# Gated linear attention and its feed-forward block: the first sequence's state held in compact form

## The chip, the cores and the metric

The kernel runs on one core of a Trainium2 chip. A core has five engines, each with an instruction queue of its own that it works through in order: TensorE (PE in the profile; PEld are its weight loads), VectorE (DVE), ScalarE (ACT), GpSimd (POOL) and SyncE (SP, which here issues every DMA). They meet only by semaphores. The metric is device time in microseconds (us), the median of several runs; smaller is better.

## The reference

Four sequences (b) of 768 tokens, 8 heads (h), 48 numbers per head. Each head carries a 48 x 48 state that decays per row by a gate f and takes in one outer product per token; the output of a token is its query times the state. The outputs, joined over the heads to 384 numbers per token, pass through a feed-forward block with a 3-tap convolution over the tokens.

```python
f = 1.0 / (1.0 + np.exp(-f_logit))
for t in range(S):
    state = f[:, :, t, :, None] * state + np.einsum('bhd,bhe->bhde', k[:, :, t], v[:, :, t])
    y[:, :, t] = np.einsum('bhd,bhde->bhe', q[:, :, t], state)
...
x = np.ascontiguousarray(attn_out.transpose(0, 2, 1, 3)).reshape(B, S, H * D)
h = np.maximum(x @ w_in, 0.0)
...
for k in range(K):
    conv_out += conv_w[k][None, None, :] * hp[:, k:k + S, :]
gate = 1.0 / (1.0 + np.exp(-conv_out))
return (h * gate @ w_out).astype(np.float32)
```

## The kernel before, in words

**Chunks.** Each sequence is cut into 6 chunks of 128 tokens; n = 0 to 23 numbers them over all four sequences, and (b, c) are the sequence and the chunk's place in it. Inside a chunk the recurrence becomes matrix products. The 8 heads go in 4 pairs p, and the two heads of a pair (j = 0, 1) lie on partitions 0 to 47 and 64 to 111. `HP` is 64, `D` is 48, `NP` is 4. On the host q and k are padded with zeros from 48 to 64 numbers per head.

**Stages of a chunk.** `gate` takes Exp and Ln of the forget logits (`fb`). `stage_a` sums them along the tokens with a triangular matmul, takes both exponentials (`fi`, `fd`, L213 and L214) and scales k and q (L226, L227). `stage_b` transposes k and q on TensorE and copies them out of PSUM (`kT`, `qT`, L251). `scores` makes the 128 x 128 score blocks (L291) and masks them with one predicated copy (`am`, L293). `state` makes the chunk's k-by-v products `pk` (L305), adds the old state (`stmp`, L315) and multiplies by the chunk's decay `ft` (L316, or L312 for the first chunk of a sequence). `values` multiplies the query block by the old state (L328) and the masked scores by v (L331) into one PSUM tile `py`, which is copied out as a high and a low part (`xT`, L339 and L340).

**The state's layout.** A state tile (`st`, two of them, `s_b[n % 2]`) has for each pair 112 columns. The head of j = 0 sits in rows 0 to 47 and columns 0 to 47, the head of j = 1 in rows 64 to 111 and columns 64 to 111; all else is zero. So one matmul of 128 rows by 112 columns per pair gives both heads' products (L328), while the update has to write the two blocks one after the other: per chunk two instructions L315 and two L316, each of 48 partitions by 192 numbers.

**The feed-forward block** is split in 8 units of half a sequence. `mm1` (L368) multiplies by w_in and does Relu, convolution and tanh on ScalarE and VectorE (L371 to L383); `mm2` (L398 to L409) splits the result into a high and a low part and multiplies by w_out (L405). The weights arrive as 64-bit floats and are split on chip (`split_f64`, L101 to L123; the tiles `mswi` and `mswo`). This happens beside the attention of the first sequence.

**What sets the order.** `plan` gives every piece a due time by hand and the pieces are recorded in that order. A scheduler then reorders the instructions of each engine by dependences and by its own estimate of the times. For chunks from n = 8 on, `visit` pins the attention's matmuls in a fixed order; before that the scheduler is free. All DMAs stand in SP's one queue: loads of k, q, v and of the logits (`load_f`, L174), the rows of the decay for later chunks (`decay_out`, `decay_in`, L233 and L241), the moves of `xT` (L345) and the output.

Of the kernel before, what the change touches and what calls it, by code (L numbers as in the profile page):

```python
# [9 lines left out]
F32 = mybir.dt.float32  # L10
# [5 lines left out]
ALU = mybir.AluOpType  # L16
PSUM = bass.MemoryType.PSUM
P = 128
# [1 line left out]
F64_HI = float(np.uint32((1151 << 20) - 1).view(np.float32))  # L20

F_MIN = 2.0 ** -64
CFG = dict(ez="ddddddaaaavvvv", ng=8, hp=4000, tb=2, groups=[3, 3, 3, 3, 3, 3, 3, 3], sg=3, f1=2.6, g1=2.6, gv=2, gl=5.2, g=3.9, l=3.2, a=1.8, b=0.8, s=0.2, v=0.5, wil=(-2.3, -1.1), wis=(-0.7, 0.9), cw=1.3, wol=(1.3, 1.0), wos=2.1, wo=0.35, m1=0.5, m1s=0.9, m2=1.5, m2s=1.2, ek=(12, 24), ec='d', er='p', tp=0, tf=2, nw=2, gd=0, q0=2, lf=3, kpool=2, eg='d', eq='p', es='d', em='d', ew='p', xb=3, nf=6, fe='a', kb=4, qb=3, vb=4, lv=2.2, cb=1, sb=3, fi=1)

@with_exitstack
def gla_moe_kernel(ctx, tc, q_in, k_in, v_in, f_in, w_in, conv_w, w_out, out):


    nc = tc.nc
    B, S, H, D = v_in.shape  # L30
    DM, DFF = w_in.shape
    q, k, v, f_logit = [t.rearrange("b s h d -> b h s d")[:, :, :, :D] for t in (q_in, k_in, v_in, f_in)]
    NC = S // P
    NP = H // 2
# [3 lines left out]
    CPH = NC // 2  # L38
    groups = CFG["groups"]
    GC = max(groups)  # L40
    first = [sum(groups[:g]) for g in range(len(groups) + 1)]
    WC = 512
    steps = [(b, c) for b in range(B) for c in range(NC)]
    HP = 64
    GAP = HP - D
# [6 lines left out]
    wk = fast.enter_context(tc.tile_pool(name="wk", bufs=2))  # L52
# [21 lines left out]
    def zeroed(shape, n, name, eng):  # L74
        ts = [wk.tile(shape, F32, name=f"{name}{i}", bufs=1) for i in range(n)]
        for t in ts:
            eng.memset(t, 0.0)
        return ts

    kp_b = [wk.tile([P, H, HP], F32, name=f"kp{i}", bufs=1) for i in range(CFG["kb"])]  # L80
    qp_b = [wk.tile([P, H, HP], F32, name=f"qp{i}", bufs=1) for i in range(CFG["qb"])]
    a_b = zeroed([P, 2, NP, P], 2, "am", nc.vector)
    s_b = zeroed([P, NP, HP + D], 2, "st", nc.vector)
# [3 lines left out]
    ft_all = const.tile([P, B, NC, NP], F32, name="ft_all")  # L87
    nc.gpsimd.memset(ft_all, 1.0)
    wi = const.tile([P, KT, 2, DFF], F32R, name="wi")
    wo = const.tile([P, NF, 2, DM], F32R, name="wo")  # L90
    cw = const.tile([P, 3, NF], F32, name="cw")

    def split_f64(raw, n, hi, lo, nm, tile=0):

        pr = raw.rearrange("p (n w) -> p n w", w=2)
        lw, hw = pr[:, :, 0], pr[:, :, 1]
        r = raw.shape[0]
        ms = wk.tile([P, 2, WC], I32, tag="gl", name=f"ms{nm}")
        m, s = ms[:r, 0, :n], ms[:r, 1, :n]
        mf, sf = m.bitcast(F32), s.bitcast(F32)  # L100
        nc.scalar.activation(mf, hw.bitcast(F32), AF.Abs)  # L101
        nc.vector.tensor_scalar(mf, mf, F64_LO, F64_HI, ALU.max, ALU.min)
        nc.vector.tensor_scalar(m, m, 1 << 27, 3, ALU.bitwise_xor, ALU.logical_shift_left)
        nc.scalar.activation(mf, mf, AF.Abs)
        nc.vector.scalar_tensor_tensor(m, hw, -(1 << 31), m, ALU.bitwise_and, ALU.bitwise_or)
        nc.vector.tensor_scalar(s, m, -(1 << 23), None, ALU.bitwise_and)
        if lo is None:
            nc.vector.scalar_tensor_tensor(sf, lw.bitcast(U32), 2.0 ** -52, sf, ALU.mult, ALU.mult)
            nc.vector.tensor_tensor(hi, mf, sf, ALU.add)
# [8 lines left out]
        nc.vector.scalar_tensor_tensor(low, lw.bitcast(U32), 2.0 ** -52, sf, ALU.mult, ALU.mult)  # L118
# [12 lines left out]

    def raw_out(f):
        i = f // 4
        if ("o", i) not in raws:
            raws["o", i] = (wk.tile([P, 4, 2 * DM], I32, tag="g32", name=f"wos{i}") if i == 0 else
                            wk.tile([P, 4, 2 * DM], I32, tag="xT", name=f"wos{i}", bufs=CFG["xb"]))
        return raws["o", i][:, f % 4]

    def load_w_in(kt, i):
        nc.sync.dma_start(raw_in(kt, i), w_in[kt * P:(kt + 1) * P, i * WC:(i + 1) * WC].bitcast(I32))  # L140

    def split_w_in(kt, i):
        cs = slice(i * WC, (i + 1) * WC)
        split_f64(raw_in(kt, i), WC, wi[:, kt, 0, cs], wi[:, kt, 1, cs], f"wi{kt}_{i}", KT * i + kt)
# [150 lines left out]
    def state(n):  # L295
        b, c = steps[n]
        if c == NC - 1:
            return
        kp, kT, qT = tts[n]
        vt = qkv[n]  # L300
        pk = ps.tile([P, NP, D], F32, tag="s", name=f"pk{n}", bufs=3)
        with visit(n - 1, 1):
            for p in range(NP):
                for j in range(2):
                    nc.tensor.matmul(pk[HP * j:HP * j + D, p, :], kp[:, 2 * p + j, :D], vt[:, 2 * p + j, :],  # L305
                                     start=True, stop=True)
        for j in range(2):
            r = slice(HP * j, HP * j + D)
            ft = ft_all[r, b, c, :].rearrange("p (n o) -> p n o", o=1).broadcast_to([D, NP, D])
            new = s_b[(n + 1) % 2][r, :, HP * j:HP * j + D]  # L310
            if c == 0:
                nc.vector.tensor_tensor(new, pk[r], ft, ALU.mult)  # L312
            else:
                tmp = wk.tile([P, NP, D], F32, tag="stmp", name=f"stmp{n}_{j}", bufs=1)
                nc.vector.tensor_tensor(tmp[r], pk[r], s_b[n % 2][r, :, HP * j:HP * j + D], ALU.add)  # L315
                (nc.vector if CFG["es"] == "d" else nc.gpsimd).tensor_tensor(new, tmp[r], ft, ALU.mult)  # L316

    def values(n):
        b, c = steps[n]
        kp, kT, qT = tts.pop(n)  # L320
        vt = qkv.pop(n)
        am = a_b[n % 2]
        py = ps.tile([P, NP, P], F32, tag="Y", name=f"py{n}")
        inter = c > 0 or n == 0
        with visit(n, 0):
            if inter:
                for p in range(NP):
                    nc.tensor.matmul(py[:HP + D, p, :], s_b[n % 2][:, p, :], qT[:, p, :], start=(p == 0), stop=False)  # L328
            for p in range(NP):
                for j in range(2):  # L330
                    nc.tensor.matmul(py[HP * j:HP * j + D, p, :], vt[:, 2 * p + j, :], am[:, j, p, :],  # L331
                                     start=not inter and p == 0, stop=(p == NP - 1))
        hf = c // CPH
        if c % CPH == 0:
            xts[b, hf] = wk.tile([P, NP, 2, HS], F32R, tag="xT", name=f"xT{b}_{hf}", bufs=CFG["xb"])
        xT = xts[b, hf]
        ts = slice((c % CPH) * P, (c % CPH + 1) * P)
        for r in [slice(0, HP + D)] if c > 0 or n == 0 else [slice(0, D), slice(HP, HP + D)]:
            nc.scalar.copy(xT[r, :, 0, ts], py[r])  # L339
            nc.vector.tensor_tensor(xT[r, :, 1, ts], py[r], xT[r, :, 0, ts].bitcast(F32), ALU.subtract)  # L340
# [133 lines left out]
    with tc.If(n_ok < P * n_ft):  # L474
        with ExitStack() as slow:
            wk = slow.enter_context(tc.tile_pool(name="swk", bufs=2))
# [13 lines left out]
            for t0 in range(0, S, TB):  # L490
# [7 lines left out]
                fb, qb, kb = grouped(f_logit, "f"), grouped(q, "q"), grouped(k, "k")  # L498
                vb = wk.tile([P, TB, D], F32, tag="sv", name=f"sv{t0}")
# [22 lines left out]
                for t in range(0, TB, 8):  # L522
                    py = ps.tile([B * H, 8, D], F32, tag="sy", name=f"spy{t0}_{t}", bufs=2)
# [14 lines left out]
            for u in range(2 * B):  # L538
                b, hf = u // 2, u % 2
# [59 lines left out]
```

## Time and profile before

| | |
|---|---|
| median of 3 runs | 376.55 us (374.24 to 377.16) |
| the profiled execution | 371.6 us, of which 369.9 us are the profile's span |
| PE busy | 346.4 us, 94% of the span |
| DVE busy | 290.4 us, 79% |
| ACT busy | 237.9 us, 64% |
| POOL busy | 53.0 us, 14% |

The span is the profile's stretch from its first to its last instruction. Busy shares are averages over stages with different limits: the first 110 us hold the weight splitting, the attention of the first sequence and the start of the feed-forward block, and only after that is TensorE filled throughout. A matmul's duration in a row holds its latency, and matmuls overlap; the busy time of a group divided by its count tells what one of them costs in a stream.

### The profile page before, as it was taken

What the parts mean: (1) busy time and instruction counts of PE and PEld (TensorE: products, weight loads), DVE (VectorE), ACT (ScalarE), POOL (GpSimd) and SP (SyncE); (2) the same over time, 40 slices, a digit from 0 to 9 for tenths busy, and PEclk for the clock granted to TensorE, in tenths of its full rate; (3) what the DMA queues carried; (4) which work ended last, traced back from release to release, by engine and by line L of the source; (5) the groups of instructions that cost most, each with busy time, mean ns of one, the idle gap of its engine ahead of it and who ended that gap; (6) DMA issues with size and microseconds to landing.
All of it is one profiled execution on the core that took longest, in us unless ns stands there. A gap on an engine that the chain in (4) does not pass through costs nothing.

```text
span 369.9 us, 7330 instructions
## 1 busy us (share of the span) xinstructions
PE 346.4 (94%) x2775; PEld 315.4 (85%) x2775; DVE 290.4 (79%) x455; ACT 237.9 (64%) x428; POOL 53.0 (14%) x72
## 2 busy tenths in 40 slices
PE   4799899989799998999999999999999999999993
PEld 1566678778699997999899999999999999999993
DVE  4799999999899877888689897689868875575620
ACT  3779777897977667567856566457464545665530
POOL 1111222112111410240101421041010000000000
PEclk9699999999999999999999999999999999999998
DMA  7999344315312450335113331341011002101011
GB/s 228 394 356 365 98 139 123 99 37 161 81 29 88 101 171 20 96 88 165 51 44 90 88 114 50 74 110 51 24 43 35 23 0 56 43 2 43 23 43 51
DMA packets 28853, 36.04 MB, mean 97 GB/s; under 512 B 10847, under 2 KB 20106, under 8 KB 28810
## 3 DMA queue, kind: packets, MB, share of 16 engines
q1 hardware_dynamic: 28810, 35.49, 32.1%
q8 instruction: 24, 0.39, 0.5%
q14 instruction: 19, 0.16, 0.1%
HBM read 28.37 MB, written 4.75 MB: 90 GB/s over the span
## 4 chain that ended last, share of the span: by engine, by line
PE 59%; ACT 14%; DVE 14%; DMA 6%; issue 4%; SPq 1%; ACTq 0%; DVEq 0%
PE po L405 23%; PE ph L368 20%; PE py L331 4%; DMA fb<-in_f_logit_dram 4%; PE pa L291 4%; PE py L328 3%; DMA wis<-in_moe_w_in_dram 2%; DVE g L379 2%; ACT fb L183 2%; DVE am L293 1%; PE ptk L249 1%; PE ptq L249 1%; PE pk L305 1%; ACT hb L371 1%; ACT g L373 1%
## 5 line engine op out<-in xcount | busy, mean ns | idle before, releaser
L368 PE MATMUL ph<-xT,wi 128*128 128x384 f32 x576 | 112.2, 344 | 4.5 <-ACT ob L408 2.5
L368 PEld LDWEIGHTS ph<-xT,wi 128*128 128x128 f32 x576 | 100.6, 188 | 8.2 <-ACT ob L408 3.7
L405 PE MATMUL po<-wo,gh 128*128 128x384 f32 x384 | 99.7, 340 | 0.2 <-ACT hb L371 0.2
L405 PEld LDWEIGHTS po<-wo,gh 128*128 128x128 f32 x384 | 69.6, 188 | 0.7 <-ACT hb L371 0.5
L405 PE MATMUL po<-wo,gl 128*128 128x384 f32 x192 | 66.0, 344 | 0.0
L379 DVE SCALAR_TENSOR_TENSOR g<-hb,cw,g 128x384 f32<-128x384 f32 (+1 forms) x64 | 43.5, 682 | 13.1 <-ACT g L373 12.5
L382 ACT ACTIVATE g<-g 128x768 f32<-128x768 f32 (+1 forms) x32 | 27.1, 848 | 38.7 <-DVE g L380 38.5
L371 ACT ACTIVATE hb<-ph 128x384 f32<-128x384 f32 x64 | 31.2, 489 | 23.5 <-PE ph L368 23.2
L380 DVE SCALAR_TENSOR_TENSOR g<-hb,cw,g 128x384 f32<-128x384 f32 (+1 forms) x64 | 41.8, 653 | 2.9
L399 DVE TENSOR_TENSOR gl<-g,gh 128x1024 fp32r<-128x1024 f32 (+4 forms) x34 | 32.2, 957 | 14.7 <-ACT gh L398 14.6
L383 DVE SCALAR_TENSOR_TENSOR g<-g,hb 128x768 f32<-128x768 f32 (+1 forms) x32 | 30.6, 957 | 14.1 <-ACT g L382 14.0
L227 POOL TENSOR_TENSOR qp<-qp,fd 128x384 f32<-128x384 f32 x22 | 28.9, 1313 | 87.7 <-ACT fd L214 72.1
L373 ACT ACTIVATE g<-hb,cw 128x384 f32<-128x384 f32 (+1 forms) x64 | 39.3, 619 | 2.2 <-ACT hb L371 0.4
L398 ACT CAST gh<-g 128x1024 fp32r<-128x1024 f32 (+4 forms) x34 | 26.5, 802 | 20.8 <-PE po L405 18.4
L405 PEld LDWEIGHTS po<-wo,gl 128*128 128x128 f32 x192 | 36.1, 188 | 1.1 <-issue 0.2
L293 DVE COPY_PREDICATED am<-mask,pa 128x1024 f32<-128x1024 uint8 x24 | 31.6, 1315 | 0.3
L291 PE MATMUL pa<-qT,kT 48*128 48x128 f32 x384 | 28.8, 286 | 0.4 <-ACT qT L251 0.4
L331 PE MATMUL py<-am,v 128*48 128x128 f32 x384 | 26.8, 277 | 1.6 <-DVE am L293 1.6
L226 DVE TENSOR_TENSOR kp<-kp,fi 128x384 f32<-128x384 f32 x22 | 22.7, 1033 | 6.8 <-ACT fi L213 6.6
L291 PEld LDWEIGHTS pa<-qT,kT 48*128 48x128 f32 x384 | 23.9, 187 | 3.8 <-issue 1.7
L331 PEld LDWEIGHTS py<-am,v 128*48 128x48 f32 x384 | 20.1, 122 | 6.8 <-DVE am L293 2.3
L328 PE MATMUL py<-qT,st 128*112 128x128 f32 x168 | 22.9, 275 | 0.1
(107 smaller groups left out, 432.1 us busy)
## 6 DMA issues: line engine op xcount, KB each, us to landing
kp<-in_k_dram SPq DMA_DIRECT2D x24, 256.0 KB
qp<-in_q_dram SPq DMA_DIRECT2D x24, 256.0 KB
fb<-in_f_logit_dram SPq DMA_DIRECT2D x24, 192.0 KB
v<-in_v_dram SPq DMA_DIRECT2D x24, 192.0 KB
out_dram<-ob SPq DMA_DIRECT2D x24, 192.0 KB
wis<-in_moe_w_in_dram SPq DMA_DIRECT2D x6, 512.0 KB
wos<-in_moe_w_out_dram SPq DMA_DIRECT2D x8, 384.0 KB
xT<-xT SPq DMA_DIRECT2D x48, 48.0 KB
```

The costliest lines, as they stand in the source:

```text
L291: nc.tensor.matmul(pa[:, j, p, :], kT[r, p, :], qT[r, p, :], start=True, stop=True)
L293: ready.setdefault(n, []).append(nc.vector.copy_predicated(am, mask, pa).ins)
L328: nc.tensor.matmul(py[:HP + D, p, :], s_b[n % 2][:, p, :], qT[:, p, :], start=(p == 0), stop=False)
L331: nc.tensor.matmul(py[HP * j:HP * j + D, p, :], vt[:, 2 * p + j, :], am[:, j, p, :], start=not inter and p == 0, stop=(p == NP - 1))
L368: nc.tensor.matmul(ph, wi[:, t, wl, f * P:(f + 1) * P], xts[b, hf][:, t, xl, :], start=(i == 0), stop=(i == 3 * KT - 1))
L371: nc.scalar.activation(hb[:, 2:HS + 2], ph, AF.Relu, scale=0.5)
L373: nc.scalar.activation(cv, hb[:, 1:n + 1], AF.Copy, scale=cw[:, 1, f:f + 1])
L379: nc.vector.scalar_tensor_tensor(cv, hb[:, 2:n + 2], cw[:, 2, f:f + 1], cv, ALU.mult, ALU.add)
L380: nc.vector.scalar_tensor_tensor(cv, hb[:, 0:n], cw[:, 0, f:f + 1], cv, ALU.mult, ALU.add)
L383: nc.vector.scalar_tensor_tensor(cv, cv, 1.0, h_b[:, fp:fp + 2, 1:n + 1], ALU.add, ALU.mult)
L399: nc.vector.tensor_tensor(lo, g[:, f:f + k], hi.bitcast(F32), ALU.subtract)
L405: nc.tensor.matmul(po, g[:, f, :], wo[:, f, wl, :], start=(i == 0), stop=(i == 3 * NF - 1))
```

## The change

For the first `CPT` = 6 chunks (a new entry cpt=6 of CFG), which are the whole first sequence, both heads' blocks of a pair are kept in the same columns 0 to 47 of the state tile, the head of j = 0 in rows 0 to 47 and that of j = 1 in rows 64 to 111.

- The update then is one instruction over all 128 partitions for both heads: one addition and one multiplication per chunk, where there were two of each (one multiplication instead of two for the first chunk). For this `pk` is made 64 columns wide, so that its unused rows hold zeros from k's padding.
- One matmul can no longer give both heads' products. Each pair takes two matmuls instead, one for each head: 48 rows by 64 columns (j = 0) and 48 rows by 48 columns (j = 1), which use opposite quarters of the array and write the partitions 0 to 63 and 64 to 111 of `py`.
- After the sixth chunk GpSimd clears the rows from 64 on in columns 0 to 47 of both state tiles. From then on the old layout is used.

```diff
+    CPT = CFG["cpt"]
...
-                    nc.tensor.matmul(pk[HP * j:HP * j + D, p, :], kp[:, 2 * p + j, :D], vt[:, 2 * p + j, :],
+                    m = HP if n < CPT else D
+                    nc.tensor.matmul(pk[HP * j:HP * j + m, p, :], kp[:, 2 * p + j, :m], vt[:, 2 * p + j, :],
                                      start=True, stop=True)
+        if n < CPT:
+            ft = ft_all[:, b, c, :].rearrange("p (n o) -> p n o", o=1).broadcast_to([P, NP, D])
+            old, new = s_b[n % 2][:, :, :D], s_b[(n + 1) % 2][:, :, :D]
+            if c > 0:
+                tmp = wk.tile([P, NP, D], F32, tag="stmp", name=f"stmp{n}", bufs=1)
+                nc.vector.tensor_tensor(tmp, pk, old, ALU.add)
+                pk = tmp
+            nc.vector.tensor_tensor(new, pk, ft, ALU.mult)
+            return
...
-            if inter:
+            if inter and n < CPT:
+                for p in range(NP):
+                    for j, m in ((0, HP), (1, D)):
+                        r = slice(HP * j, HP * j + D)
+                        nc.tensor.matmul(py[HP * j:HP * j + m, p, :], s_b[n % 2][r, p, :m], qT[r, p, :],
+                                         start=(p == 0), stop=False)
+            elif inter:
...
+        if n == CPT - 1:
+            for t in s_b:
+                nc.gpsimd.memset(t[HP:, :, :D], 0.0)
```

The scheduler makes a new order of the first part of the program from this; from about the second row block of the feed-forward output on (`po_1`), TensorE's order is nearly the same again. Line numbers of the changed kernel are higher: L314 and L316 are its additions and multiplications of the compact state, L341 its quarter-array matmuls, L402 the tanh (L382 before), L184 and L185 the Exp and Ln of the gate (L183 and L184 before).

VectorE, the update after the second chunk (n = 1), with the weight splitting (`mswi`, `lowwi`) around it, before:

```order
L293 COPY_PREDICATED am_96<-mask_86,pa_332 128x1024
L105 SCALAR_TENSOR_TENSOR mswi_1_342<-wis_152,mswi_1_342 128x512
L315 TENSOR_TENSOR stmp_0_386<-pk_377,st_100 48x192
L105 SCALAR_TENSOR_TENSOR mswi_1_362<-wis_152,mswi_1_362 128x512
L106 TENSOR_SCALAR mswi_1_342<-mswi_1_342 128x512
L316 TENSOR_TENSOR st_99<-stmp_0_386,ft_all 48x4x48
L106 TENSOR_SCALAR mswi_1_362<-mswi_1_362 128x512
L118 SCALAR_TENSOR_TENSOR lowwi_1_350<-wis_152,mswi_1_342 128x512
L315 TENSOR_TENSOR stmp_1_389<-pk_377,st_100 48x192
L118 SCALAR_TENSOR_TENSOR lowwi_1_370<-wis_152,mswi_1_362 128x512
L340 TENSOR_TENSOR xT_0_310<-py_447,xT_0_310 112x4x128
L316 TENSOR_TENSOR st_99<-stmp_1_389,ft_all 48x4x48
```

The same place now:

```order
L294 COPY_PREDICATED am_96<-mask_86,pa_335 128x1024
L106 SCALAR_TENSOR_TENSOR mswi_1_345<-wis_152,mswi_1_345 128x512
L314 TENSOR_TENSOR stmp_389<-pk_380,st_100 128x192
L106 SCALAR_TENSOR_TENSOR mswi_1_365<-wis_152,mswi_1_365 128x512
L107 TENSOR_SCALAR mswi_1_345<-mswi_1_345 128x512
L316 TENSOR_TENSOR st_99<-stmp_389,ft_all 128x4x48
L107 TENSOR_SCALAR mswi_1_365<-mswi_1_365 128x512
L119 SCALAR_TENSOR_TENSOR lowwi_1_353<-wis_152,mswi_1_345 128x512
L119 SCALAR_TENSOR_TENSOR lowwi_1_373<-wis_152,mswi_1_365 128x512
```

The two instructions of the second head (`stmp_1`, and the second write of `st_99`) are gone, and the others stand as they stood.

ScalarE, where the feed-forward block's first tanh meets the gate of the fifth group of chunks (`fb_1091`, now `fb_1104`), before. An ACT_TABLE_LOAD changes between the function set with Exp and Ln and the one with tanh:

```order
L183 ACTIVATE fb_1091<-fb_1091 128x1152
L371 ACTIVATE hb<-ph_2_753 128x384
L251 COPY kT_920<-ptk_915 128x512
L184 ACTIVATE fb_1091<-fb_1091 128x1152
L251 COPY qT_927<-ptq_922 128x512
L104 ACTIVATE mswo_783<-mswo_783 128x384
L373 ACTIVATE g_689<-hb,cw 128x384
L213 ACTIVATE fi_932<-pl_929 128x384
L214 ACTIVATE fd_931<-pl_929 128x384
L101 ACTIVATE mswo_851<-wos_357 128x384
L382 ACT_TABLE_LOAD
L382 ACTIVATE g_689<-g_689 128x2x384
```

Now:

```order
L184 ACTIVATE fb_1104<-fb_1104 128x1152
L359 CAST xT_1_681<-py_839 112x4x128
L402 ACT_TABLE_LOAD
L402 ACTIVATE g_695<-g_695 128x2x384
L185 ACT_TABLE_LOAD
L185 ACTIVATE fb_1104<-fb_1104 128x1152
L391 ACTIVATE hb<-ph_4_876 128x384
L402 ACT_TABLE_LOAD
L402 ACTIVATE g_695<-g_695 128x2x384
```

The first tanh now stands between this gate's Exp and its Ln, so there are two ACT_TABLE_LOADs more: ten in the whole program, where there were eight.

SyncE, the loads of the same group's logits, before:

```order
L174 DMA fb_1091<-in_f_logit_dram 128x384 x2
L233 DMA ft_862<-fd_825 1x384
L174 DMA fb_1091<-in_f_logit_dram 128x384
L241 DMA ft_all<-ft_862 48x4x1 x2
```

Now:

```order
L175 DMA fb_1104<-in_f_logit_dram 128x384 x3
L203 DMA v_1009<-in_v_dram 128x384
L234 DMA ft_869<-fd_828 1x384
L242 DMA ft_all<-ft_869 48x4x1 x2
```

The third of the three loads no longer stands behind the store of a decay row (`ft_862`), which reads the result of an exponential (`fd_825`) of ScalarE.

More of the change, by code (lines that the diff above doesn't have):

```diff
@@ L22 @@
 F_MIN = 2.0 ** -64
-CFG = dict(ez="ddddddaaaavvvv", ng=8, hp=4000, tb=2, groups=[3, 3, 3, 3, 3, 3, 3, 3], sg=3, f1=2.6, g1=2.6, gv=2, gl=5.2, g=3.9, l=3.2, a=1.8, b=0.8, s=0.2, v=0.5, wil=(-2.3, -1.1), wis=(-0.7, 0.9), cw=1.3, wol=(1.3, 1.0), wos=2.1, wo=0.35, m1=0.5, m1s=0.9, m2=1.5, m2s=1.2, ek=(12, 24), ec='d', er='p', tp=0, tf=2, nw=2, gd=0, q0=2, lf=3, kpool=2, eg='d', eq='p', es='d', em='d', ew='p', xb=3, nf=6, fe='a', kb=4, qb=3, vb=4, lv=2.2, cb=1, sb=3, fi=1)
+CFG = dict(ez="ddddddaaaavvvv", ng=8, cpt=6, hp=4000, tb=2, groups=[3, 3, 3, 3, 3, 3, 3, 3], sg=3, f1=2.6, g1=2.6, gv=2, gl=5.2, g=3.9, l=3.2, a=1.8, b=0.8, s=0.2, v=0.5, wil=(-2.3, -1.1), wis=(-0.7, 0.9), cw=1.3, wol=(1.3, 1.0), wos=2.1, wo=0.35, m1=0.5, m1s=0.9, m2=1.5, m2s=1.2, ek=(12, 24), ec='d', er='p', tp=0, tf=2, nw=2, gd=0, q0=2, lf=3, kpool=2, eg='d', eq='p', es='d', em='d', ew='p', xb=3, nf=6, fe='a', kb=4, qb=3, vb=4, lv=2.2, cb=1, sb=3, fi=1)
 @with_exitstack
```

## The prediction

> **What bounds the kernel now.** I read the engines' busy time in stretches first, because a share over the whole span mixes stages. Columns: the stretch, its length, then the busy time of PE, PEld, DVE, ACT and POOL with counts, TensorE's granted clock, and the DMA engines' share and rate.
>
> ```profile
> 20.00:30.00 10.00, 9.44 (x111) 6.82 (x109) 9.74 (x19) 8.94 (x21) 1.10 (x2) 1.00 1.01 361
> 30.00:40.00 10.00, 9.63 (x110) 6.95 (x110) 9.78 (x23) 8.97 (x22) 2.12 (x2) 1.00 0.78 278
> 40.00:50.00 10.00, 8.85 (x93) 6.39 (x92) 9.69 (x23) 6.38 (x17) 1.91 (x1) 1.00 0.40 98
> 50.00:60.00 10.00, 10.00 (x87) 7.56 (x86) 9.30 (x20) 8.94 (x18) 1.06 (x1) 1.00 0.60 158
> 70.00:80.00 10.00, 8.75 (x72) 7.46 (x72) 9.49 (x18) 9.60 (x17) 1.83 (x2) 1.00 0.19 40
> 80.00:90.00 10.00, 10.00 (x79) 8.71 (x79) 9.94 (x19) 9.40 (x19) 1.59 (x2) 1.00 0.57 152
> 200.00:300.00 100.00, 99.63 (x848) 95.69 (x845) 84.06 (x123) 56.43 (x99) 16.05 (x20) 1.00 0.23 62
> ```
>
> From 20 to 60 us VectorE is busy 38.5 of 40 us. PE looks as full, but its durations hold latency; its weight loads, 6.4 to 7.6 of 10, tell that it has room. After 200 us PEld is at 95.7%, and TensorE sets the pace. What is gained or lost before about 110 us is therefore carried to the end whole: behind it there is TensorE work of unchanged amount, in nearly unchanged order.
>
> The chain of waits between 25 and 64 us says the same of the first stage, and names the rows that the change touches:
>
> ```profile
> by line: issue 11.6%; DVE mswo L103 11.0%; DVE st L316 7.6%; DVE am L293 7.3%; DVE mswo L105 6.7%; DVE stmp L315 6.4%; DVE mswo L102 4.1%; DVE lowwi L118 3.4%; DVE mswi L105 3.3%; DVE mswo L106 3.0%; ACT fi L213 3.0%; ACT mswi L101 3.0%; DV
> ...
> 34.42 0.37 DVE stmp L315
> ...
> 61.49 0.37 DVE st L316
> ```
>
> State updates are 14.0% of these 39 us. The two rows are the first and the last of seven pieces of 0.36 or 0.37 us that are updates of the second head; its other two updates (one of the first chunk, one of the second) lie beside ScalarE's part of the chain.
>
> From 64 us to 112 us the chain is mixed:
>
> ```profile
> by line: PE ph L368 17.9%; DMA fb<-in_f_logit_dram 12.6%; PE po L405 9.5%; ACT g L373 5.9%; DVE mswo L103 5.9%; issue 5.4%; ACT L382 5.3%; ACT hb L371 5.0%; ACT fb L183 4.9%; ACT g L382 3.5%; ACT L184 2.7%; PE pa L291 2.4%; ACT qT L251 2.2%
> ```
>
> **VectorE: nine instructions fewer.** Groups between 15 and 64 us, by shape (count, busy, mean ns):
>
> ```profile
> L316 DVE TENSOR_TENSOR st<-stmp,ft_all 48x192 f32<-48x192 f32 x8 | 3.6, 452 | 0.1
> L315 DVE TENSOR_TENSOR stmp<-pk,st 48x192 f32<-48x192 f32 x8 | 2.8, 352 | 0.1
> L312 DVE TENSOR_TENSOR st<-pk,ft_all 48x192 f32<-48x192 f32 x2 | 0.7, 352 | 0.0
> ```
>
> Of 2 + 8 + 8 instructions 1 + 4 + 4 stay. I take the merged one as costing what one of 48 partitions costs: the instruction walks the same 192 numbers, and in the same trace the wider L340 (112 partitions, 681 ns) and its 48-partition form (687 ns) cost the same:
>
> ```profile
> L340 DVE TENSOR_TENSOR xT<-py,xT 112x512 fp32r<-112x512 f32 x21 | 14.3, 681 | 1.9 <-ACT xT L339 1.7
> L340 DVE TENSOR_TENSOR xT<-py,xT 48x512 fp32r<-48x512 f32 x6 | 4.1, 687 | 0.1
> ```
>
> A removed instruction frees more than its 0.36 us, as VectorE's rows in order of time show. The first three surround a second head's addition, the last three a first head's:
>
> ```profile
> 40.79 1.28 DVE L293 COPY_PREDICATED am<-mask,pa 128x1024 f32<-128x1024 uint8 x1
> 42.10 0.36 DVE L315 TENSOR_TENSOR stmp<-pk,st 48x192 f32<-48x192 f32 x1
> 42.50 0.36 DVE L106 TENSOR_SCALAR mswo<-mswo 128x384 int32<-128x384 int32 x1
> ...
> 44.85 0.35 DVE L102 TENSOR_SCALAR mswo<-mswo 128x384 f32<-128x384 f32 x1
> 45.12 0.34 DVE L315 TENSOR_TENSOR stmp<-pk,st 48x192 f32<-48x192 f32 x1
> 45.38 0.54 DVE L226 TENSOR_TENSOR kp<-kp,fi 128x384 f32<-128x384 f32 x1
> ```
>
> The first head's addition starts 0.08 us before its forerunner ends (44.85 + 0.35 = 45.20) and its successor 0.08 us before it ends itself. The second head's starts 0.03 us after 42.07, and its successor 0.04 us after it. Without it L106 could start 0.08 us before 42.07, at 41.99 and not at 42.50: 0.51 us per removed instruction. Nine of them are 4.6 us of VectorE's queue; the seven on the chain are 7 x 0.51 = 3.6 us. **I take 3.6 us; the ends are 0 (another engine is then just as late) and 4.6 us.**
>
> **ScalarE: two more table loads.** The order shows them around the second tanh. The group of L382, then the three loads that the chain of 64 to 112 us holds:
>
> ```profile
> L382 ACT ACT_TABLE_LOAD x3 | 3.8, 1283 | 0.1
> ```
>
> ```profile
> 76.09 1.28 ACT L382
> ...
> 93.88 1.28 ACT L184
> ...
> 96.86 1.28 ACT L382
> ```
>
> 2 x 1.28 = 2.6 us more. All three loads that the chain of before meets up to 112 us stand on it at full length, and ACT is busy 19.0 of the 20 us from 70 to 90 us. I take +2.6 us; if they fall into ScalarE's waits it is 0.
>
> **SyncE: the logits' loads.** ScalarE waits for them twice, and the chain of 64 to 112 us holds both:
>
> ```profile
> 67.53 0.26 SPq L233
> ...
> 67.83 2.44 DMA fb<-in_f_logit_dram
> ...
> 88.02 3.59 DMA fb<-in_f_logit_dram
> ```
>
> At 67.5 us the third load of `fb_1091` stood behind the store L233. That store is now behind the three loads, so this wait goes. ScalarE idled before the two gates for
>
> ```profile
> 70.37 1.17 ACT L183 ACTIVATE fb<-fb 128x1152 f32<-128x1152 f32 x1 [0.94 <-DMA fb<-in_f_logit_dram]
> 91.71 1.17 ACT L183 ACTIVATE fb<-fb 128x1152 f32<-128x1152 f32 x1 [1.56 <-DMA fb<-in_f_logit_dram]
> ```
>
> 0.94 and 1.56 us. I count the first, -0.9 us, and not the second; the ends are 0 and -2.5 us.
>
> **TensorE: 48 matmuls in place of 24.** Each is two instructions (fp32), so 16 per chunk for 8, in six chunks. The nearest rows:
>
> ```profile
> L291 PE MATMUL pa<-qT,kT 48*128 48x128 f32 x384 | 28.8, 286 | 0.4 <-ACT qT L251 0.4
> L331 PE MATMUL py<-am,v 128*48 128x128 f32 x384 | 26.8, 277 | 1.6 <-DVE am L293 1.6
> L328 PE MATMUL py<-qT,st 128*112 128x128 f32 x168 | 22.9, 275 | 0.1
> ```
>
> Busy time by count is 75 ns for the scores (48 rows), 70 ns for the products with v (48 columns) and 136 ns for the full form: the two heads of a pair run side by side in the half-array forms. If the quarters do too, a chunk costs 16 x 0.070 to 16 x 0.075 = 1.12 to 1.20 us against 8 x 0.136 = 1.09, at most +0.1; six chunks +0.2 to +0.7 us, of which I count 0.4. If they take turns, it is 16 x 0.136 = 2.18 us a chunk and +6.5 us in all. No row has two tiles of different rows in one PSUM tile: the scores of the two heads go to different halves of `pa`, the products with v share the rows.
>
> The Trainium skill, "TensorEngine Tiling (Array Packing)", section "Restrictions and Gotchas", says that different row tiles write to different PSUM banks and cannot use the same bank simultaneously; a bank holds 512 fp32 values by "PSUM — Partial Sum Buffer", section "Specifications (TRN2)", which is all of `py`, so by this rule they take turns. Against that, "TensorE: Matmul & The Clock Gate", section "Why this matters for your kernels", has row and column tiles composing with one bank per row of tiles. No run here shows which holds for opposite quarters. By the first the sum below is 6.1 us higher.
>
> **The rest** costs nothing. The 16 added columns of `pk` lengthen a weight load at most from 124 ns to the 144 ns of a 128-column one:
>
> ```profile
> L305 PEld LDWEIGHTS pk<-v,kp 128*48 128x48 f32 x320 | 10.3, 124 | 3.6 <-issue 1.7 <-DVE c L109 0.5 <-ACT kT L251 0.4
> L249 PEld LDWEIGHTS ptk<-ident,kp 128*128 128x128 f32 x96 | 12.0, 144 | 3.8 <-issue 2.0 <-DVE kp L226 0.8
> ```
>
> 80 of them by 20 ns are 1.6 us of PEld in a stage where PEld has 2.4 to 3.6 us free in each 10; without that cover it is 1.6 us. The two clearings stand in POOL's queue ahead of the scaling of q for later chunks, and wait for the last product with the compact state. Each of 192 numbers lies between
>
> ```profile
> L359 POOL MEMSET hb<- 128x4 f32 x16 | 1.5, 104 | 52.8 <-DVE g L383 52.8
> L77 DVE MEMSET st<- 128x448 f32 x2 | 0.9, 432 | 0.1
> ```
>
> 0.10 and 0.43 us, on an engine busy 1.8 of 10 us there; uncovered, 0.9 us for both.
>
> **The sum.** -3.6 + 2.6 - 0.9 + 0.4 = -1.5 us. The profiled execution's own time is 371.6 us and becomes 370.1. It lies 5.0 us below the median of the runs shown, 376.55, so I put the same difference on the median: 375.0 us.
>
> **The rivals.**
>
> *B, the table loads are covered.* ScalarE has 3.6 us free between 40 and 50 us and waits 2.5 us for the two gates; if VectorE's earlier end lets it start earlier, the loads fall into such waits. Then -3.6 - 0.9 + 0.4 = -4.1, and with all nine instructions and both waits gone -4.6 - 2.5 + 0.4 = -6.7: 369.9 to 372.5 us. For it: the loads of `fb` now stand earlier in SP's queue. Against it: all three loads of before lie on the chain.
>
> *C, the quarters take turns (slower).* One mechanism, in `py` of the chunks 0 to 5: +6.5 for +0.4 gives -1.5 + 6.1 = +4.6, 381.2 us. It decides as far as TensorE has no room: with half of it absorbed (PEld is free 2.4 to 3.6 us in 10) it is +1.5 us, 378.1 us. Against it: heads that share columns or rows already run side by side, and opposite quarters share neither.
>
> *D, the gain is taken back (slower, or no change).* VectorE comes early, but ScalarE, busy 8.9 us in three of the four stretches from 20 to 60 us, is as late, and the gates don't come earlier. Then 0 + 2.6 + 0.4 = +3.0 us, 379.6 us; with half of the 3.6 us kept +1.2, 377.8 us. For it: two of the nine removed instructions already lie beside ScalarE's chain. Against it: ScalarE idles 3.6 us between 40 and 50 us.
>
> One stall can go either way in each case. VectorE's L103, in order of time (the second row is GpSimd's group of the split of the gates),
>
> ```profile
> 61.88 2.83 DVE L103 TENSOR_SCALAR mswo<-mswo 128x384 int32<-128x384 int32 x1
> ```
>
> ```profile
> L189 POOL TENSOR_TENSOR cgl<-fb,cgh 128x1152 fp32r<-128x1152 f32 x5 | 13.2, 2650 | 21.9 <-PE ph L368 14.2 <-ACT cgh L188 7.7
> ```
>
> has the length of GpSimd's L189, where L106 above, of the same kind and size, takes 0.36 us. In the new order another instruction may meet it, so 2.5 us more or less; that is inside the range.
>
> **How the numbers follow.** The forecast has a chance of 0.41, B 0.22, C 0.16, D 0.21. The forecast's own range is 372.5 to 377.5. For 8 in 10 I go down to 370.5, into B, and up to 380.0, past all of D and the milder half of C; its harsh half and B's far end are left out. One per cent, about what a measurement of this kernel can tell from no change, is 3.8 us: faster is below 372.8, slower above 380.3. Faster gets most of B and a tenth of the forecast, 0.22. Slower gets half of C, a fifth of D and a few hundredths of the forecast for the moved stall, 0.15. Between them 0.63.
>
> **What will show it.** L314 and L316 at about 0.35 us, five and four of them, and the first sequence's last state update, at 61.5 us before, about 4 us earlier: right on VectorE. L341 busy near 0.07 us per instruction: the quarters run side by side; near 0.136: C. Ten ACT_TABLE_LOADs, two more on the chain between 70 and 90 us: right on ScalarE; if they end idle time instead, B. No wait for `fb` at the fifth group's Exp: right on SyncE. It would be wrong altogether if the chain up to 64 us left VectorE, or if the tail after 112 us, which I took as unchanged, became longer or shorter.

## The result, and the profile after

The changed kernel takes 380.38 us (median of 14 runs, 377.98 to 381.21), the kernel before 374.99 us (14 runs beside it, 373.37 to 377.16). The ratio is 1.0119, with a 95% interval of 1.0095 to 1.0143: about 1.2% or some 5 us slower. The forecast was 375.0 us, 1.5 us below the 376.55 us that 3 runs of the kernel before had then given. That the kernel before itself now has 374.99 us is chance. Disturbed executions are left out of the ratios, so a ratio can differ a little from that of the two medians beside it.

The profiled execution of the changed kernel took 379.46 us (span 377.7), 7.9 us more than that of before. Some 2 of these 7.9 us are not the change's. Up to the scores of chunk 0 on TensorE, and up to the mask behind them on VectorE, the instructions are the same in both programs and in the same order, and that mask already starts 2.2 us later. First before, then after:

```profile
19.32 1.30 DVE L293 COPY_PREDICATED am<-mask,pa 128x1024 f32<-128x1024 uint8 x1
```

```profile
21.56 1.30 DVE L294 COPY_PREDICATED am<-mask,pa 128x1024 f32<-128x1024 uint8 x1
```

The rows of the stretch ahead of it (stretch, length, busy time of PE, PEld, DVE, ACT, POOL, granted clock, DMA share and rate) show TensorE at another granted clock. First before, then after:

```profile
10.00:20.00 10.00, 8.34 (x57) 5.88 (x58) 8.18 (x15) 7.17 (x16) 1.40 (x1) 0.74 1.04 394
```

```profile
10.00:20.00 10.00, 7.53 (x36) 4.84 (x38) 6.25 (x12) 6.95 (x15) 1.40 (x1) 0.55 1.01 352
```

0.74 and 0.55 of full speed: one execution's luck, for in the profiles of the first two experiments below, both in the order of before, it is 0.51 and 1.00. The medians, not the two profiles, say what the change costs. To compare starts between profiles, I count them from chunk 0's mask.

Later stretches of after, to be read beside the prediction's first fence:

```profile
30.00:40.00 10.00, 9.89 (x111) 6.46 (x107) 8.85 (x20) 9.11 (x23) 2.12 (x2) 1.00 0.94 333
50.00:60.00 10.00, 10.00 (x79) 5.98 (x79) 7.33 (x17) 7.06 (x17) 0.84 (x1) 1.00 0.47 115
...
80.00:90.00 10.00, 9.46 (x96) 7.30 (x95) 7.18 (x12) 9.34 (x16) 2.31 (x4) 1.00 0.14 41
90.00:100.00 10.00, 5.87 (x48) 4.92 (x46) 8.04 (x15) 4.91 (x9) 1.53 (x2) 0.83 0.44 107
...
200.00:300.00 100.00, 99.64 (x862) 95.92 (x861) 82.82 (x120) 58.22 (x104) 16.99 (x20) 1.00 0.25 67
```

In the first two of these stretches VectorE, at 9.78 and 9.30 of 10 us before, is at 8.85 and 7.33 now: it has become lighter, and it waits. The end is unchanged (PEld 95.92 of 100). The hole is new: from 90 to 100 us TensorE is busy 5.87 us, at a granted clock of 0.83. TensorE's rows in order of time, and the end of the chain that leads there, show why:

```profile
84.72 2.54 PE L388 MATMUL ph<-xT,wi 128*128 128x384 f32 x12
...
94.49 2.26 PE L388 MATMUL ph<-xT,wi 128*128 128x384 f32 x6 [4.13 <-DMA xT<-xT]
```

```profile
90.07 0.47 DVE mswo L114
90.54 0.47 DVE mswo L115
91.00 0.60 DVE xT L360
91.60 0.48 DVE wo L116
92.08 0.07 SPq L365
...
92.20 2.16 DMA xT<-xT
...
94.49 2.26 PE ph L388 x6
```

The first matmul of unit 1 waits 4.13 us for the moves of `xT` within SBUF. They wait for chunk 5's low part (L360), which in VectorE's queue stands behind the splitting of an output weight (L114, L115). Before, unit 1 began without such a wait:

```profile
86.05 0.44 PE L368 MATMUL ph<-xT,wi 128*128 128x384 f32 x1
```

Counted from chunk 0's mask, unit 1 begins at 72.9 us now (94.49 - 21.56) and began at 66.7 us before (86.05 - 19.32). These 6.2 us are already the whole loss (the medians differ by 5.4). And the hole costs more than its length. Six matmuls take 2.26 us there, where twelve took 2.54 us at 84.72. Columns as above (the granted clock is the third from the right), for four single microseconds:

```profile
94.00:95.00 1.00, 0.51 (x2) 0.54 (x3) 1.00 (x1) 0.00 (x0) 0.00 (x0) 0.50 0.47 86
96.00:97.00 1.00, 1.00 (x4) 0.88 (x3) 0.97 (x2) 0.00 (x0) 0.00 (x0) 0.50 0.61 128
97.00:98.00 1.00, 1.00 (x5) 0.68 (x4) 0.00 (x1) 0.17 (x1) 0.00 (x0) 0.79 0.89 281
98.00:99.00 1.00, 1.00 (x15) 0.76 (x15) 0.56 (x1) 1.00 (x3) 0.22 (x1) 1.00 0.62 193
```

After the wait the matmuls run at half speed until about 97.4 us.

VectorE's own rows of after: the merged updates, in groups by shape between 15 and 64 us, and the first sequence's last update in order of time:

```profile
L316 DVE TENSOR_TENSOR st<-stmp,ft_all 128x192 f32<-128x192 f32 x3 | 1.1, 352 | 0.0
L314 DVE TENSOR_TENSOR stmp<-pk,st 128x192 f32<-128x192 f32 x3 | 1.0, 346 | 0.0
```

```profile
73.18 0.34 DVE L316 TENSOR_TENSOR st<-stmp,ft_all 128x192 f32<-128x192 f32 x1
```

An update over 128 partitions costs what one over 48 did, 0.35 us, as the prediction took it. But the last one stood at 61.49 us before and was to come some 4 us earlier; it starts at 73.18 us, 9.5 us later counted from the mask. The instructions are saved, and the time isn't.

ScalarE's table loads, in order of time:

```profile
75.77 1.16 ACT L184 ACTIVATE fb<-fb 128x1152 f32<-128x1152 f32 x1
77.42 1.28 ACT L402 ACT_TABLE_LOAD   x1
...
79.57 1.28 ACT L185 ACT_TABLE_LOAD   x1
...
82.43 1.28 ACT L402 ACT_TABLE_LOAD   x1
```

Three within 6.3 us where there was one, all three in the chain of 64 to 112 us. The Exp at 75.77 us has no wait for `fb` any more, yet it stands 5.4 us later than before's (70.37), 3.2 us counted from the mask.

TensorE's quarter products, both forms apart, then together, in after:

```profile
L341 PE MATMUL py<-qT,st 48*64 48x128 f32 x48 | 7.8, 282 | 0.0
L341 PE MATMUL py<-qT,st 48*48 48x128 f32 x48 | 7.6, 278 | 0.0
```

```profile
L341 PE MATMUL py<-qT,st 48*48 48x128 f32 (+1 forms) x96 | 8.8, 280 | 0.0
```

7.8 and 7.6 us apart, 8.8 us together: the two quarters of a pair run side by side, although both write one PSUM tile.

### The profile page after: what moved, and what is told of

The parts are those of the page before. It is cut to its first block, busy times and chain, and to the rows that moved or that the text cites. A ratio compares the mean times of both kernels' runs of the same rounds, so it can differ in the third digit from the quotient of the medians.

```text
span 377.7 us, 7415 instructions
## 1 busy us (share of the span) xinstructions
PE 355.3 (94%) x2823; PEld 318.2 (84%) x2823; DVE 287.1 (76%) x446; ACT 241.2 (64%) x430; POOL 51.3 (14%) x74
## 4 chain that ended last, share of the span: by engine, by line
PE 68%; DVE 11%; ACT 9%; DMA 7%; issue 2%; SPq 1%; ACTq 0%; DVEq 0%
PE po L425 22%; PE ph L388 21%; PE pa L292 5%; PE py L348 5%; PE py L345 3%; DVE g L400 3%; DMA kp<-in_k_dram 2%; DMA wis<-in_moe_w_in_dram 2%; PE pl L210 2%; DVE g L399 2%; PE ptk L250 2%; PE ptq L250 2%; DVE kp L227 2%; PE pk L307 2%; ACT fb L184 1%
## 5 line engine op out<-in xcount | busy, mean ns | idle before, releaser
L388 PE MATMUL ph<-xT,wi 128*128 128x384 f32 x576 | 113.6, 346 | 7.5 <-DMA xT<-xT 4.1
L402 ACT ACTIVATE g<-g 128x768 f32<-128x768 f32 (+1 forms) x32 | 27.1, 847 | 39.9 <-DVE g L400 39.8
L399 DVE SCALAR_TENSOR_TENSOR g<-hb,cw,g 128x384 f32<-128x384 f32 (+1 forms) x64 | 42.5, 669 | 13.1 <-ACT g L393 12.5
L400 DVE SCALAR_TENSOR_TENSOR g<-hb,cw,g 128x384 f32<-128x384 f32 (+1 forms) x64 | 45.5, 712 | 2.9
L228 POOL TENSOR_TENSOR qp<-qp,fd 128x384 f32<-128x384 f32 x22 | 27.6, 1256 | 98.6 <-ACT fd L215 86.8
L292 PE MATMUL pa<-qT,kT 48*128 48x128 f32 x384 | 30.3, 287 | 0.1
L348 PE MATMUL py<-am,v 128*48 128x128 f32 x384 | 27.9, 278 | 0.0
L359 ACT CAST xT<-py 112x512 fp32r<-112x512 f32 (+1 forms) x27 | 15.7, 580 | 8.0 <-PE py L348 5.2
```

The lines of the kernel that those rows point to most:

```text
L292: nc.tensor.matmul(pa[:, j, p, :], kT[r, p, :], qT[r, p, :], start=True, stop=True)
L388: nc.tensor.matmul(ph, wi[:, t, wl, f * P:(f + 1) * P], xts[b, hf][:, t, xl, :], start=(i == 0), stop=(i == 3 * KT - 1))
L399: nc.vector.scalar_tensor_tensor(cv, hb[:, 2:n + 2], cw[:, 2, f:f + 1], cv, ALU.mult, ALU.add)
L400: nc.vector.scalar_tensor_tensor(cv, hb[:, 0:n], cw[:, 0, f:f + 1], cv, ALU.mult, ALU.add)
```

## The experiments

Two theories were set against each other. **ORDER**: the scheduler, given other instructions, placed the rest of the work differently, and that costs the time. **FORM**: the quarter products themselves cost TensorE. To part them, an order can be imposed: behind the whole recording, a table lists each engine's instructions, and each is told to issue behind its forerunner. A new instruction takes the place of the one that it replaces.

```diff
+ORDER = {
...
+}
+def pinned(tc, nc, order, mybir):
+    nosync = mybir.DependencyInfo(mybir.DependencyClass.NoSync, mybir.DependencyReason.DATA)
+    mine = [i for i in nc.cur_bb.bb.instructions if type(i).__name__.startswith("Inst")]
+    for e, runs in order.items():
+        own = [i for i in mine if str(i.engine).split(".")[-1] == e]
+        row = [own[k] for a, b in runs for k in range(a, b)]
+        for x, y in zip(row, row[1:]):
+            tc.add_manual_dep(y, x.name, nosync, reason="pinned")
...
+    pinned(tc, nc, ORDER, mybir)
     n_ft = B * NC * NP
```

### Form and order apart

**Both parts of the change, old order** (the diff above in the changed kernel, with before's table):

> The changed kernel's instructions (one update over 128 partitions for each of chunks 0 to 5, quarter products), pinned on every engine to the order that the kernel before has; each new instruction stands where the one that it replaces stood. Theory ORDER (the 5.4 us are lost because the scheduler placed chunks 4 and 5 later, three table loads close together and the first matmuls of unit 1 ahead of their data): with the old order the loss is gone, 371 to 375 us against 375 of the kernel before, and the wait of some 4 us ahead of the first matmul of unit 1 is gone. Theory FORM (the quarter products cost TensorE time at each change of tile shape, 0.09 to 0.18 us each, and this stands on the path from 20 to 62 us): 378 to 381 us, as the changed kernel.

373.15 us, ratio to the kernel before 0.9947 (0.9920 to 0.9975): the same change, faster by 0.5%. ORDER holds. Chunk 0's mask, the last update of the first sequence and unit 1's first matmul, which has no wait:

```profile
22.28 1.30 DVE L309 COPY_PREDICATED am<-mask,pa 128x1024 f32<-128x1024 uint8 x1
...
60.55 0.35 DVE L331 TENSOR_TENSOR st<-stmp,ft_all 128x192 f32<-128x192 f32 x1
```

```profile
86.80 0.44 PE L403 MATMUL ph<-xT,wi 128*128 128x384 f32 x1
```

Counted from the mask the last update comes at 38.3 us (42.2 before) and unit 1 at 64.5 us (66.7 before): 3.9 and 2.2 us earlier.

**The update alone, old order** (the state products stay full-array matmuls over the compact tile, as many and as large as before; what the kernel leaves out is the second head's part of these products in chunks 0 to 5):

```diff
-            if inter and n < CPT:
...
-            elif inter:
+            if inter:
```

> Only the update over 128 partitions, in the old order on every engine; the state products stay full-array matmuls over the compact tile (the second head's part of the product is then left out of chunks 0 to 5). Both theories expect a gain or nothing: 371 to 375 us, since VectorE has 9 operations fewer and no tile shape is added. A loss here would mean that the update itself, not the products, costs time.

372.97 us, ratio 0.9939 (0.9919 to 0.9959): -0.6%, some 2.3 us.

**The products alone, old order** (the updates and the memory of the state stay as before; the edit is shown against the kernel before):

```diff
-            if inter:
+            if inter and n < CPT:
+                for p in range(NP):
+                    for j, m in ((0, HP), (1, D)):
+                        r = slice(HP * j, HP * j + D)
+                        nc.tensor.matmul(py[HP * j:HP * j + m, p, :], s_b[n % 2][r, p, HP * j:HP * j + m], qT[r, p, :],
+                                         start=(p == 0), stop=False)
+            elif inter:
...
```

> Only the quarter products, in the old order; the state keeps its two diagonal blocks in 112 columns and is updated by head as before. Theory ORDER: within 1 us of the kernel before (374 to 376). Theory FORM: 378 to 383 us, the changed kernel's loss and the gain of VectorE not taken.

374.50 us, ratio 0.9981 (0.9959 to 1.0002). The quarters cost nothing that these runs can tell; FORM falls. Their row here is 7.3 us for 96 instructions, 0.076 us each:

```profile
L347 PE MATMUL py<-qT,st 48*48 48x128 f32 (+1 forms) x96 | 7.3, 278 | 0.0
```

**The kernel before in the new order**, with a table made of the changed kernel's order (an operation that was one and is two or more again stands at its place):

```diff
+ORDER = {
...
+}
...
+    pinned(tc, nc, ORDER, mybir)
     n_ft = B * NC * NP
```

> The kernel before's instructions (update by head, full products), pinned on every engine to the order of the changed kernel. Theory ORDER: 379 to 383 us, with two more table loads and the wait ahead of the first matmul of unit 1. Theory FORM: 374 to 377 us.

379.77 us, ratio 1.0117 (1.0089 to 1.0146): all of the loss, without one changed instruction. The wait ahead of unit 1 is there, and chunk 5's low part at the same time as in the changed kernel (90.93):

```profile
94.21 2.26 PE L383 MATMUL ph<-xT,wi 128*128 128x384 f32 x6 [4.13 <-DMA xT<-xT]
```

```profile
90.65 0.68 DVE L355 TENSOR_TENSOR xT<-py,xT 112x512 fp32r<-112x512 f32 x1
```

So in the old order the form is worth 0.5%, and in the new order nothing, 1.0119 against 1.0117.

### What in the order costs

**SPLITS or TABLES?** Two due times of the changed kernel, with the scheduler free, so that other instructions move too (of the line only the two entries are shown):

```diff
-... wos=2.1, wo=0.35 ...
+... wos=3.0, wo=0.45 ...
```

> The changed kernel, order left to the scheduler; two of its due times are changed: the splitting of the output weights starts at 3.0 chunks instead of 2.1 and goes on by 0.45 instead of 0.35. In VectorE's order the number of these splitting operations that stand ahead of the masks of chunks 3, 4 and 5 falls from 17, 31 and 43 to 10, 20 and 32 (kernel before: 10, 22 and 33); the ten table loads stay. Theory SPLITS (the new order puts some ten half-microsecond splits ahead of chunks 3 to 5, so that the first half's output is late and the first matmul of unit 1 waits): 372 to 376 us, the wait of 4 us gone. Theory TABLES (the two added table loads and what they hold up on ScalarE): 378 to 381 us.

378.13 us, ratio 1.0075 (1.0045 to 1.0104). Neither theory alone: the ten loads stay and so does more than half of the loss, but 0.4% is gone by the two ratios. The wait for `xT` shrank from 4.13 to 0.71 us; smaller waits remain ahead of it, and the clock drops all the same (six matmuls in 2.26 us):

```profile
85.44 0.66 PE L250 MATMUL ptq<-ident,qp 128*128 128x128 f32 x4 [0.78 <-POOL qp L228]
87.30 1.28 PE L210 MATMUL pl<-fb,tri 128*128 128x384 f32 x2 [1.21 <-ACT kT L252]
89.29 2.26 PE L388 MATMUL ph<-xT,wi 128*128 128x384 f32 x6 [0.71 <-DMA xT<-xT]
```

**The splits still later**:

```diff
-... wos=2.1, wo=0.35 ...
+... wos=3.4, wo=0.35 ...
```

> As e5_splits_later, with the splitting of the output weights from 3.4 chunks on (by 0.35): 10, 15 and 27 splitting operations ahead of the masks of chunks 3, 4 and 5, fewer than in the kernel before. Theory SPLITS: as e5_splits_later or up to 1.5 us faster, 371 to 375 us, unless the splits then come late for the second product (its first matmul waits for wo). Theory TABLES: 378 to 381 us.

378.85 us median with a wide spread (375.85 to 382.6), against 375.19 of the kernel before beside it: 1.0098 by the two medians, and a ratio of 1.0044 (1.0013 to 1.0076). No better than the one above with any certainty. That the splits stand early is not the whole cause; the theory SPLITS, which wanted 371 to 375 us, falls as a whole.

**The two table loads**: the first experiment, with one move on ScalarE.

```diff
-L185 Ln of gate 4
...
 L402 first tanh
+L185 Ln of gate 4
```

> The changed kernel's instructions in the old order, as e1_both_old_order, with one move: on ScalarE the logarithm of gate 4 stands behind the first tanh instead of ahead of it, which adds two table loads. Theory TABLES: 2.5 us or more over e1_both_old_order, 375.7 us or more. Theory SPLITS: 0 to 1 us over it, 373 to 374.2 us, since ScalarE has idle time around the first tanh.

376.01 us, ratio 1.0007 (0.9974 to 1.0040), against 0.9947 without the move: +0.6% (0.2 to 1.0 by the two intervals), some 2.2 us for two loads of 1.28 us. The move also puts the Ln itself eight places later, and this run doesn't part the two. The loads' rows:

```profile
74.61 1.28 ACT L417 ACT_TABLE_LOAD   x1
76.77 1.28 ACT L200 ACT_TABLE_LOAD   x1
85.35 1.28 ACT L417 ACT_TABLE_LOAD   x1
```

**The wait partly filled**: the changed kernel in its own order, with nine matmuls of TensorE's queue put ahead of unit 1's first.

```diff
+pl8, pk7
 ph1_0 x3, ph1_1 x3
-pl8
 ph1_0 x3, ph1_1 x3
-pk7
```

> The changed kernel in its own order on every engine, but on TensorE the prefix sum of chunk 8 and the key product of chunk 7, which stand behind the first matmuls of unit 1, are put ahead of them, so that some 1.1 us of the 4.1 us wait is filled. If that wait is the loss itself, 378.5 to 379.5 us against 380.4 of the changed kernel; if TensorE's wait there is only a symptom of a late chunk chain, no change (380 to 381).

377.28 us, ratio 1.0058 (1.0034 to 1.0082), against 1.0119: -0.6%, some 2.3 us for 1.1 us of moved work, more than either theory expected; but the two intervals leave 1.0 to 3.6 us. Chunk 0's mask, the first moved matmuls (unit 1 follows them without a wait of its own), and eighteen matmuls of unit 1 further on, which stand at 103.54 us in the changed kernel:

```profile
20.24 1.30 DVE L309 COPY_PREDICATED am<-mask,pa 128x1024 f32<-128x1024 uint8 x1
```

```profile
91.71 1.02 PE L225 MATMUL pl<-fb,tri 128*128 128x384 f32 x2 [2.64 <-ACT kT L267]
...
101.03 3.43 PE L403 MATMUL ph<-xT,wi 128*128 128x384 f32 x18
```

Counted from the mask these eighteen are 1.2 us earlier (80.8 against 82.0), about the moved work. The clock is no part of the gain: it stands at 0.50 for as long behind this wait as in the changed kernel (3.4 us from 92.4 us on). Behind the prefix sum (L225) hang ScalarE's two exponentials of chunk 8, and with them the chunk's whole chain; in the changed kernel it stood behind matmuls that waited for something else. Whether that gives more than the filled wait is not shown.

**Both undone in the new order**, the loads and the wait. The move on TensorE is that of the run above, and on ScalarE:

```diff
+L185 Ln of gate 4
 L402 first tanh
-L185 Ln of gate 4
```

> The changed kernel in its own order, with the move of e7_hole_filled on TensorE and one on ScalarE: the logarithm of gate 4 stands one place earlier, ahead of the first tanh, which takes the two added table loads away. If the two costs add up (0.6% each, as e6 against e1 and e7 against the changed kernel measured them), a ratio of 1.000 to the kernel before, about 375 us; if the loads lie beside the late chunk chain in this order, as e7_hole_filled, 377 us.

375.05 us, ratio 1.0000 (0.9957 to 1.0043), the number expected of a plain sum. Two moves, of one instruction on ScalarE and nine on TensorE, take back the whole loss, as far as the interval tells. Against the run above, the loads alone are again worth 0.6% (0.1 to 1.1), here by one place on ScalarE.

**The kernel before's instructions in that mended order** (the compact updates and quarter products undone, the table kept):

```diff
-CFG = dict(ez="ddddddaaaavvvv", ng=8, cpt=6,
...
+CFG = dict(ez="ddddddaaaavvvv", ng=8,
...
```

> The kernel before's instructions (update by head, full products) in the order of e9_hole_and_loads: the changed kernel's order without the two added table loads and with the wait partly filled. e9 with the compact form measured a ratio of 1.000. If the compact form is worth 0.5% in this order too, as it is in the old one, 1.005 here, 377 us; if the late chunk chain leaves it nothing, as e4 against the changed kernel says, 1.000 here too, 375 us.

375.85 us, ratio 1.0041 (1.0014 to 1.0068). Once the loads and the wait are out of the way, the compact form shows a gain again, 0.4% by the two ratios; their intervals overlap, so this is likely, not shown. What is left of the new order costs the form of before 0.4%.

### A version that beats both

In the old order TensorE waits 2.33 us for a copy that stands on ScalarE behind the fourth tanh and its table load, and then runs slowly:

```profile
101.92 0.69 PE L225 MATMUL pl<-cgh,tri 128*128 128x384 f32 x1 [2.33 <-ACT kT L267]
```

```profile
102.00:103.00 1.00, 1.00 (x4) 0.51 (x4) 1.00 (x4) 1.00 (x3) 0.00 (x0) 0.50 0.03 8
...
107.00:108.00 1.00, 1.00 (x5) 1.00 (x5) 0.97 (x3) 0.48 (x1) 1.00 (x1) 0.50 0.00 2
108.00:109.00 1.00, 1.00 (x8) 0.74 (x8) 1.00 (x1) 0.00 (x0) 0.12 (x1) 0.69 0.03 0
```

The two copies of chunk 8 were put ahead of that tanh on ScalarE, first with the changed kernel's instructions, then with before's:

```diff
+L252 COPY kT8, qT8
 L402 tanh
...
-L252 COPY kT8
-L252 COPY qT8
```

> The changed kernel's instructions in the old order, as e1_both_old_order, and on ScalarE the two copies of the transposed k and q of chunk 8 stand ahead of the fourth tanh and its table load instead of behind it. In the profile of e1 TensorE waits 2.3 us there for the first of them and then runs some 7 us at a granted clock of 0.5. If that wait and the slow stretch behind it are worth their length, 370 to 372 us; if TensorE only waits a little later, 373 us as e1.

> The same move of the two copies in the kernel before (its own instructions, otherwise its own order). 373 to 375 us: a gain of the same kind as in e10, or none, as TensorE's wait there (2.2 us) had no slow stretch behind it in the profile. The compact form is worth 2 us more if e10 lies 2 us below this run, as e1 lay below the kernel before.

372.43 us, ratio 0.9930 (0.9898 to 0.9962), and 374.48 us, ratio 0.9978 (0.9947 to 1.0009). The first is the fastest kernel of all by its median, 0.7% ahead of the kernel before, but from the first experiment's 0.9947 it can't be told apart: TensorE just waits later, for the halves of the second product, and the clock falls behind that wait too, for half as long:

```profile
103.81 0.62 PE L440 MATMUL po<-wo,gh 128*128 128x384 f32 x2 [2.38 <-ACT gh L433]
```

```profile
106.00:107.00 1.00, 1.00 (x13) 0.56 (x13) 1.00 (x2) 1.00 (x3) 0.22 (x1) 0.50 0.00 0
```

Between the two runs the form is again worth 0.5%.

## Why the prediction was wrong, point by point

**The order, the step that failed.** The sum has four terms, and of the new order it holds two table loads and one store. All else that the scheduler moved in the first 110 us was put at nothing, and without a reason: "The rest" weighs weight loads and clearings alone. Before's instructions alone, in the new order, lose 1.17% (0.89 to 1.46), some 4.4 us. The two loads make about half of that (2.2 us, below); the other half is the missing term. What it does shows at unit 1: its first matmul starts 6.2 us later, counted from chunk 0's mask, with 4.13 us of idle TensorE ahead of it and half speed behind it. The other half of the step held: behind about 110 us the work is as it was, and what was lost ahead of it came through to the end (6.2 us at unit 1, 5.4 us by the medians).

The condition named for being wrong altogether was met: the chain up to 64 us left VectorE. Its shares in after:

```profile
by line: PE pzwi L121 10.0%; PE py L348 9.9%; PE pa L292 9.8%; PE py L341 9.2%; PE pzwo L121 8.1%; PE pl L210 7.7%; PE ptk L250 5.6%; PE ptq L250 5.3%; ACT fb L184 5.1%; PE pk L307 4.7%; PE pzwo L122 3.8%; PE pl L219 3.6%; PE pzwo L123 3.3%
```

But this sign was a poor one. In the first experiment, which is faster than the kernel before, the chain lies on TensorE as well:

```profile
by line: PE pa L307 10.5%; PE pzwi L136 9.8%; PE py L356 8.5%; PE py L363 8.0%; PE pzwo L136 7.6%; PE pl L225 7.6%; PE pk L322 7.1%; PE ptk L265 5.6%; PE ph L403 4.6%; PE ptq L265 4.5%; issue 4.3%; DVE am L309 3.2%; PE pzwo L138 2.8%; PE pl
```

**VectorE, -3.6 us.** The terms were right: nine instructions fewer, 0.35 us each. In the old order the last update does come 3.9 us earlier, unit 1 only 2.2 us, and the update alone is worth 0.6%, 2.3 us by 375 (1.5 to 3.0): two thirds of the 3.6. Where the rest is lost on the way is not shown. In the new order next to nothing is left: chunk 5's low part comes at 90.65 us with the old updates and at 90.93 us with the new ones, 70.1 and 69.4 us counted from their masks (at 20.53 and 21.56).

**ScalarE, +2.6 us.** Right, and right in place: 0.6%, 2.2 us (0.6 to 3.9), measured in the old order, and 0.6% again in the new one. Rival B, loads that are covered, falls.

**SyncE, -0.9 us.** Both waits for `fb` are gone from the rows, but so is their meaning: the gate whose wait went starts 5.4 us later than before, 3.2 us counted from the mask. The term did not arrive. No run tested it alone.

**TensorE's quarters, +0.4 us.** Right by the time: -0.2% with an interval that reaches 0. Busy, they take 0.092 us each in the changed kernel (8.8 us by 96) and 0.076 us with the products alone in the old order; the forecast was 0.070 to 0.075. The 48 full products that they replace take 6.5 us at 0.136, so the busy time grew by 2.3 and 0.8 us; in the old order that cost nothing that shows, in the new one no run tests it alone. Rival C, by which each was to take 0.136 us, falls: the Trainium skill's "TensorEngine Tiling (Array Packing)", section "Restrictions and Gotchas", by which row tiles cannot use one PSUM bank simultaneously, does not hold for these opposite quarters (7.8 and 7.6 us apart, 8.8 us together, in one tile). The "one bank per row of tiles" that the prediction set against that rule asks for the same; what speaks against it is this run, where two rows of tiles share one bank.

**Rival D, the gain taken back**, came nearest: 377.8 to 379.6 us were given for it, 380.38 were measured. It had the loads and the lost gain, but named ScalarE's load as the cause and had no TensorE wait. The range ended at 380.0 us.

**The moved stall** of VectorE beside GpSimd's split of the gates did move, and kept its size: 3.00 us at another instruction.

```profile
67.85 3.00 DVE L400 SCALAR_TENSOR_TENSOR g<-hb,cw,g 128x384 f32<-128x384 f32 x1
```

**The account by the runs**, in per cent of 375 us, each uncertain by 0.3 to 0.5: the form -0.5 (first experiment), the two loads +0.6, the order of the nine matmuls around the wait +0.6, the rest of the new order +0.4 (before's form in the mended order). That is +1.1, against +1.2 measured. It isn't exact in every corner: for before's form the last three add up to 1.6, and 1.17 (0.89 to 1.46) was measured. With loads and wait in place the form's gain doesn't show. What within the order makes chunks 3 to 5 late beyond the splits stays open.

## What to carry to other kernels

Where a scheduler orders the work, a change of a few instructions is two changes, and the larger may be the order. Hold the order fixed to price the change, then read the new order for itself: on each in-order queue, which instruction can be stuck, and what that others wait for is queued behind it. A saving on a full engine is worth its time only if the next stage's first instruction also comes earlier; look for that instruction's start, not for the busy share.

## What the runs showed of the hardware

A short wait of TensorE can cost more than its length. Between 60 and 112 us of the profiles, the granted clock fell to 0.50 behind 4.13 us (changed kernel, and the kernel before in its order) and behind nine of eleven waits of 2.06 to 2.91 us; with the splits later it fell behind 0.78 and 1.21 us close together. At one and the same place it fell behind 2.33 us (first experiment), and did not behind 2.23 us (the kernel before) and 2.09 us (the update alone). Added up from the clock by the microsecond, the stretches at 0.50 are 3.4 us long (eight, with the changed kernel's from 94.0 to 97.4 us) or 6.8 us (four, with the first experiment's from 101.8 to 108.6 us), nothing between. Where TensorE sets the pace, half of that is lost, by estimate 1.7 or 3.4 us.

The Trainium skill's "TensorE: Matmul & The Clock Gate", section "Part 1: The HAM clock gate (the "warmup" mystery)", gives half rate after at least one idle window of about 3.4 us, with windows that run freely. The half rate agrees, and the stretches are of one and two such lengths; waits shorter than a window were enough here. That about the same wait has this tail in one profile and not in another may be one reason why executions of the kernel before spread from 373.37 to 377.16 us; this was not tested.

The quarters' price depends on their neighbours: the same 96 instructions are busy 8.8 us in the changed order, where they stand in more pieces among full-array matmuls, and 7.3 us in the old one, in the first experiment as with the products alone. That the changes of shape are what costs is not shown.
